# x loaded behind the first quarter of wq, and the last rows of wo in smaller pieces, in a DMA-bound attention kernel

## The chip, the cores and the metric

The kernel runs on one core of one Trainium2 chip. The metric is device microseconds of one execution. Runs of this kernel scatter by a few tenths of a microsecond (363.38 to 363.65 in the first three), so every experiment was run in five rounds beside runs of the kernel before, on the same chip. All runs told of here are fast, with a granted TensorE clock of 1.00 (0.995 at least). A ratio is the mean time of one kernel's fast runs over that of the kernel before in the same rounds, so it is not quite the ratio of the medians that are quoted. In the profiles PE is TensorE (PEld its weight loads), DVE VectorE, ACT ScalarE, POOL GpSimd, and SP the engine that issues the loads; a load is said to have landed when the last step of its semaphore stands in the trace (the kernel before starts on row 28 of wo at 356.86 us, 0.05 us after its landing at 356.81).

## The reference

Grouped-query attention over a cache, with its projections:

```python
# x (32, 4, 1024), k_cache and v_cache (32, 4, 2048, 128), wq (1024, 4096), wo (4096, 1024), all bf16
q = (x @ wq).reshape(B, Sq, Hq, Dh).transpose(0, 2, 1, 3)      # Hq = 32, Dh = 128
k = jnp.repeat(k_cache, 8, axis=1); v = jnp.repeat(v_cache, 8, axis=1)
p = softmax(einsum("bhqd,bhkd->bhqk", q, k) * Dh ** -0.5)
o = einsum("bhqk,bhkd->bhqd", p, v)
return o.transpose(0, 2, 1, 3).reshape(B, Sq, Hq * Dh) @ wo
```

About 151 MB have to be read (64 loads of 2 MB for k and v, 8 MB each for wq and wo), and 128 tokens are all that they are used for.

## The kernel before

All loads are issued from one queue (SP), in program order. First x and the four quarters of wq; x is transposed on TensorE, and the q projection takes one quarter of wq after another:

```python
p.dma("sp", lambda e: e.dma_start(x_sb, x_flat[:, :]), [], "x", "s_x")
wq_v = wq.rearrange("(p a) n -> p a n", p=128)
for c in range(4):
    p.dma("sp", lambda e, c=c: e.dma_start(w_sb[:, 2 * c:2 * c + 2, :], wq_v[:, 2 * c:2 * c + 2, :]),
          [], ("wq", c), f"s_w{c}")
# ... then the loads of k and v, each when its buffer is free
```

x is 256 KB, 2 KB a partition; a quarter of wq is 2 MB, 16 KB a partition. The v buffers lie where wq lies, so the first v load waits for the q projection.

At the end come 32 "rows" of wo (a row is 256 KB, the 128x1024 block of wo for one head), in pieces of up to four rows, into buffers that k and v leave. `WO` counts the rows of a piece; the last row, number 31, comes in two halves of its columns:

```python
WO = (4, 4, 4, 4, 4, 4, 2, 2, 2, 1)
pieces = [(sum(WO[:c]), m, 0, D) for c, m in enumerate(WO)] + [(Hq - 1, 1, 0, NA), (Hq - 1, 1, NA, D)]
# ...
def oproj(u):                        # for u in range(32): two matmuls a row, 512 columns each
    for j, (at, n0, n1) in enumerate(COLS):
        # ... matmul ps_s[:, at:...] += oT(u).T @ wo_row(u)[:, n0:n1]
        piece = next(c for c, (v, m, a, z) in enumerate(pieces) if v <= u < v + m and a <= n0 and n1 <= z)
        p.op("pe", mm, [("wo", piece), ("ot", B - 1)], ("op", j) if u == Hq - 1 else None)
```

A matmul may start when its whole piece has landed. Then ACT and DVE copy a half of the result each, and two DMAs store them.

## Time and profile before

Median 363.38 us. The page's rows of 40 slices: the DMA row is the mean busy share of the 16 DMA engines in tenths, the other what they moved.

```profile
DMA  8999999999999999999999999999999999999995
GB/s 328 429 431 433 429 428 420 431 428 428 425 422 435 426 429 424 432 428 431 426 424 435 425 431 424 429 431 429 429 424 431 429 429 424 428 433 428 412 414 197
```

The engines are busy, 9 tenths or more, from the second slice to the last but one. So the time is the start of the stream, plus the bytes at about 427 GB/s, plus what comes after the last bytes. Loads are issued long before they land, as the table of DMA issues shows (size, then microseconds from issue to landing):

```profile
big<-in_wo_dram SPq DMA_DIRECT2D x6, 1024.0 KB, 22.8
big<-in_wo_dram SPq DMA_DIRECT2D x3, 512.0 KB, 24.5
P_sb<-in_x_dram SPq DMA_DIRECT2D x1, 256.0 KB, 2.7
big<-in_wo_dram SPq DMA_DIRECT2D x1, 256.0 KB, 21.8
big<-in_wo_dram SPq DMA_DIRECT2D x2, 128.0 KB, 19.1
```

Two stretches of the timeline matter. Its columns are start, duration, engine, line, operation and tiles, count, and in brackets the idle time before it and what ended that. First the start:

```profile
0.74 0.38 SPq L186 DMA_DIRECT2D P_sb<-in_x_dram  x1
1.17 1.86 SPq L189 DMA_DIRECT2D big<-in_wq_dram  x4
3.47 1.07 PE L243 MATMUL ps_r<-ident,P_sb 128*128 128x128 bf16 x8 [3.47 <-DMA P_sb<-in_x_dram]
...
8.67 0.59 PE L262 MATMUL ps_r<-big,P_sb 128*128 128x512 bf16 x1 [4.12 <-DMA big<-in_wq_dram]
...
23.26 0.39 PE L262 MATMUL ps_r<-big,P_sb 128*128 128x512 bf16 x1 [1.26 <-DMA big<-in_wq_dram]
...
26.92 0.33 SPq L210 DMA_DIRECT2D big<-in_v_cache_dram  x1
```

PE can start on x at 3.47 us and on the first quarter of wq at 8.67, once each has landed (at 3.43 and 8.53); it waits for the last quarter, too. Then the end. L418 is the matmul of a row's first 512 columns, L16 (a helper) that of the second 512; row 28 starts at 356.86:

```profile
356.06 0.38 PE L418 MATMUL ps_s<-big,KT_sb 128*128 128x512 bf16 x1
356.27 0.38 PE L16 MATMUL ps_s<-big,KT_sb 128*128 128x512 bf16 x1
356.85 0.33 PEld L418 LDWEIGHTS ps_s<-big,KT_sb 128*128 128x128 bf16 x2 [0.91 <-DMA big<-in_wo_dram]
356.86 0.39 PE L418 MATMUL ps_s<-big,KT_sb 128*128 128x512 bf16 x1 [0.21 <-DMA big<-in_wo_dram]
...
357.73 0.38 PE L418 MATMUL ps_s<-big,KT_sb 128*128 128x512 bf16 x1
...
358.38 0.38 PE L16 MATMUL ps_s<-big,KT_sb 128*128 128x512 bf16 x1
358.58 0.60 ACT L427 ACTIVATE P_sb<-ps_s 128x512 bf16<-128x512 f32 x1 [16.24 <-PE ps_s L418]
358.80 0.69 DVE L428 CAST P_sb<-ps_s 128x512 bf16<-128x512 f32 x1 [16.12 <-PE ps_s L16]
```

Matmuls overlap: they start every 0.215 us, though each is shown as 0.38. Row 27 could have been followed at 356.49 (356.27 + 0.215), and row 28 starts 0.37 us after that, when its piece has landed. From there eight matmuls run without a further wait.

### The profile page before, as it was taken

The numbers are of one execution on the slowest core, as the hardware profiler recorded it, in microseconds if no ns is written. First come the engines' busy times: TensorE is split into PE (matmuls) and PEld (weight loads), VectorE is DVE, ScalarE is ACT, GpSimd is POOL, SyncE is SP. The second block draws the span as 40 slices with busy tenths as digits, with TensorE's granted clock in tenths as the row PEclk, the third lists the DMA queues.
The fourth block names the chain that finished last, engine by engine and source line by source line (L and its number), as shares of the span: only waits on it lengthen the run. The fifth ranks groups of instructions, "written<-read, shape, count | busy, mean of one in ns | idle before, by whom it ended". The sixth has DMA issues, their size and how long they took to land. (4 is left out here: it accounts for less than half of the span.)

```text
span 361.8 us, 6210 instructions
## 1 busy us (share of the span) xinstructions
PE 307.2 (85%) x2998; PEld 146.8 (41%) x2338; DVE 269.1 (74%) x170; ACT 102.7 (28%) x110; POOL 165.3 (46%) x262
## 2 busy tenths in 40 slices
PE   1988788999989999988999888888888889889896
PEld 1002000454445544444445444444333344449711
DVE  0018799999899898879998888888888888856500
ACT  1014222333333333333333333333322223333000
POOL 8002055355555555554455444445555554444000
PEclk9999999999999999999999999999999999999999
DMA  8999999999999999999999999999999999999995
GB/s 328 429 431 433 429 428 420 431 428 428 425 422 435 426 429 424 432 428 431 426 424 435 425 431 424 429 431 429 429 424 431 429 429 424 428 433 428 412 414 197
DMA packets 11963, 151.66 MB, mean 419 GB/s; under 512 B 1328, under 2 KB 1840, under 8 KB 2480
## 3 DMA queue, kind: packets, MB, share of 16 engines
q1 hardware_dynamic: 11808, 151.39, 98.7%
q8 instruction: 6, 0.10, 0.1%
q10 hardware_dynamic: 144, 0.13, 0.1%
q14 instruction: 5, 0.04, 0.0%
HBM read 151.26 MB, written 0.26 MB: 419 GB/s over the span
## 5 line engine op out<-in xcount | busy, mean ns | idle before, releaser
L327 DVE STREAM_TRANSPOSE KT_sb<-big 128x2048 f32<-128x2048 f32 x64 | 146.6, 2293 | 16.8 <-DMA big<-in_k_cache_dram 16.8
L353 ACT ACTIVATE P_sb<-ps_s,negmx 128x2048 bf16<-128x2048 f32 x32 | 82.0, 2564 | 185.0 <-DVE negmx L349 185.0
L16 PE MATMUL ps_s<-KT_sb,QD_sb 128*128 128x512 bf16 x384 | 103.7, 377 | 0.0
L384 POOL COPY PD_sb<-PT_sb 32x1024 f32<-32x1024 f32 x62 | 64.1, 1034 | 63.4 <-PE ps_r L393 60.6
L384 POOL COPY big<-PT_sb 32x1024 f32<-32x1024 f32 x61 | 63.0, 1034 | 59.1 <-PE ps_r L393 56.3
L349 DVE TENSOR_REDUCE negmx<-ps_s 128x1 f32<-128x2048 f32 x32 | 73.2, 2286 | 12.4 <-PE ps_s L16 10.9
L393 PE MATMUL ps_r<-big 128*128 128x128 bf16 x1024 | 59.8, 219 | 11.3 <-PEq L85 11.3
L393 PE MATMUL ps_r<-big,PD_sb 128*128 128x128 bf16 x1024 | 59.8, 219 | 9.9 <-PEq L85 9.9
L393 PEld LDWEIGHTS ps_r<-big 128*128 128x128 bf16 x1024 | 57.9, 98 | 22.1 <-issue 21.6
L393 PEld LDWEIGHTS ps_r<-big,PD_sb 128*128 128x128 bf16 x1024 | 58.0, 98 | 21.2 <-issue 20.7
L340 PE MATMUL ps_s<-KT_sb,QD_sb 128*128 128x512 bf16 x128 | 48.3, 377 | 18.3 <-PEq L85 18.3
L340 PEld LDWEIGHTS ps_s<-KT_sb,QD_sb 128*128 128x128 bf16 x128 | 12.3, 96 | 103.1 <-issue 103.1
L362 DVE STREAM_TRANSPOSE PT_sb<-P_sb 128x1024 f32<-128x1024 f32 x32 | 39.8, 1245 | 15.8 <-ACT P_sb L353 15.8
L317 POOL COPY QD_sb<-QT_sb 32x64 f32<-32x64 f32 x128 | 29.4, 229 | 46.1 <-DVE QT_sb L296 20.4
L16 PE MATMUL ps_r<-ident 128*128 128x384 bf16 x173 | 33.3, 325 | 0.0
L365 PEld LDWEIGHTS ps_r<-ssum,permf 128*128 128x128 f32 x64 | 11.9, 187 | 24.8 <-issue 23.1
L402 ACT ACTIVATE QT_sb<-ps_r,rinv 128x128 bf16<-128x128 f32 x32 | 11.7, 367 | 29.5 <-PE ps_r L393 27.3
L278 DVE TENSOR_SCALAR KT_sb<-ps_r 128x512 bf16<-128x512 f32 x2 | 1.3, 686 | 20.1 <-PE ps_r L262 20.1
L16 PE MATMUL ps_s<-big,KT_sb 128*128 128x512 bf16 x32 | 12.1, 379 | 1.2 <-DVE KT_sb L409 1.1
L428 DVE CAST P_sb<-ps_s 128x512 bf16<-128x512 f32 x1 | 0.7, 691 | 16.1 <-PE ps_s L16 16.1
L418 PE MATMUL ps_s<-big,KT_sb 128*128 128x512 bf16 x30 | 11.4, 381 | 1.4 <-DMA big<-in_wo_dram 1.4
L251 PE MATMUL ps_r<-ident 128*128 128x384 bf16 x32 | 10.3, 322 | 0.0
(41 smaller groups left out, 85.3 us busy)
## 6 DMA issues: line engine op xcount, KB each, us to landing
big<-in_k_cache_dram SPq DMA_DIRECT2D x32, 2048.0 KB, 18.6
big<-in_v_cache_dram SPq DMA_DIRECT2D x32, 2048.0 KB, 22.1
big<-in_wq_dram SPq DMA_DIRECT2D x4, 2048.0 KB, 14.0
big<-in_wo_dram SPq DMA_DIRECT2D x6, 1024.0 KB, 22.8
big<-in_wo_dram SPq DMA_DIRECT2D x3, 512.0 KB, 24.5
P_sb<-in_x_dram SPq DMA_DIRECT2D x1, 256.0 KB, 2.7
big<-in_wo_dram SPq DMA_DIRECT2D x1, 256.0 KB, 21.8
big<-in_wo_dram SPq DMA_DIRECT2D x2, 128.0 KB, 19.1
```

Source lines behind the costliest of these rows:

```text
L16: return eng.add_instruction(mybir.InstMatmult(name=nc.get_next_instruction_name(), engine=eng.engine, start_tensor_calc=start, stop_tenso ...
L317: p.op("pool", lambda e, s=src, d=dst: e.tensor_copy(d, s), waits if g == 0 else [("pt", i - 2)] * (g == 1 and i > 1), ("qd", i) if g == G ...
L327: p.op("dve", lambda e, s=src, d=dst: e.transpose(d, s), waits, ("kt", i, c), gives="t_kt" if c else None)
L340: mm = lambda e, a_=(out_, lhsT, rhs), f=first, l=last: e.matmul(a_[0], lhsT=a_[1], rhs=a_[2], start=f, stop=l, skip_group_check=True)
L349: p.op("dve", lambda e: e.tensor_reduce(negmx[:, i % 4:i % 4 + 1], ps_s[:, :], AX.X, ALU.max, negate=True), [("qk", i)], ("negmx", i))
L353: p.op("act", lambda e: e.activation(P_sb[:, :, :, :].rearrange("p t r w -> p t w r"), ps_s[:, :].rearrange("p (t w r) -> p t w r", w=2, r=R),
L362: p.op("dve", lambda e: e.transpose(dst, src), [("exp", i)], ("pt", i))
L365: p.op("pe", lambda e: e.matmul(ring[(i if i == L else i // 2 * 2) % 4][:, 510 + i % 2:511 + i % 2], lhsT=permf[:, :], rhs=ssum[:, i % 4:i ...
L384: p.op("dve" if i >= B - 2 and g < i - B + 4 else "pool", lambda e, s=src, d=dst: e.tensor_copy(d, s), [free] * (g == 0 or i >= B - 2) + [ ...
L393: p.op("pe", lambda e: e.matmul(buf[:, 0:Dh], lhsT=pd_of(i)[:, t // 2, :, :, :, t % 2].rearrange("p x g q -> p (x g q)"), rhs=big[:, slot_ ...
L402: p.op("act", lambda e: e.activation(dst, src, ACT.Copy, scale=rinv[:, i % 4:i % 4 + 1]), [("pv", i), ("rinv", i)], ("o", i))
L418: mm = lambda e, a=(out_, lhsT, rhs): e.matmul(a[0], lhsT=a[1], rhs=a[2], start=(u == 0), stop=(u == Hq - 1), skip_group_check=True)
```

## The change

The intent: start the stream with the large load that the q projection needs first, and let row 28 start when its own 256 KB are there instead of those of row 29 as well.

```diff
-    WO = (4, 4, 4, 4, 4, 4, 2, 2, 2, 1)
+    WO = (4, 4, 4, 4, 4, 4, 2, 2, 1, 1, 1)
 ...
-        p.dma("sp", lambda e: e.dma_start(x_sb, x_flat[:, :]), [], "x", "s_x")
         wq_v = wq.rearrange("(p a) n -> p a n", p=128)
         for c in range(4):
             p.dma("sp", lambda e, c=c: e.dma_start(w_sb[:, 2 * c:2 * c + 2, :], wq_v[:, 2 * c:2 * c + 2, :]),
                   [], ("wq", c), f"s_w{c}")
+            if c == 0:
+                p.dma("sp", lambda e: e.dma_start(x_sb, x_flat[:, :]), [], "x", "s_x")
```

Nothing else moves: on every other engine the instructions and their order are the same, and SP issues one DMA more.

## The prediction

> **What bounds the kernel now.** The DMA engines. The page's row of slices shows the mean DMA share at 9 tenths or more from the second slice to the second last, at 412 to 435 GB/s; PE is busy 85%, DVE 74%. The queue never runs dry: wo pieces land 19 to 24 us after issue (table of DMA issues). So the time is: start of the stream + bytes at about 427 GB/s + what follows the last bytes. Fine windows put the first large completions at 2.3 us and the last bytes at 357.6 us of a 361.8 us span. The chain that ended last agrees: a wo DMA until 356.81, then 1.7 us of matmuls, the copy, the store.
>
> **The end.** The timeline shows the output projection waiting for pieces of wo: row 27 ends its issue near 356.49 (0.215 us a matmul, two a row), row 28 begins at 356.86, when the 512 KB piece of rows 28 and 29 has landed. From there eight matmuls run at their own pace: no further wait. The change splits that piece into two of 256 KB. [...] The previous 512 KB piece landed 1.28 us before this one, so half of it is an estimated 0.6 us: row 28 lands near 356.25, before PE wants it (356.49). Row 29 lands near 356.85 to 356.95, PE wants it at 356.92. Bytes stop at 357.6, so the last halves are there for 357.8 and 358.0. Gain: 0.3 to 0.37 us, all on the chain. Cost: one more issue (about 0.4 us on SP, 17 us ahead of need, free) and 2 KB instead of 4 KB runs for 512 KB, under 0.1 us.
>
> **The start.** x (256 KB) is issued at 0.74 us, wq at 1.17 us; both at full rate: x's bytes and the first wave of wq's 16 KB packets complete back to back (473 KB between 2.3 and 3.1 us), so x in front leaves no visible hole. Moving it behind the first wq load moves the same bytes; I give it 0 us, within 0.3 either way (better start with large packets, or x no longer hidden in the start-up).
>
> On the compute side it costs: x now lands near 8.7 us instead of 3.45. Transposes (1.07 us) and the copy (0.69 us) follow, so the q projection starts near 10.6 instead of 8.67. PE then catches up: it used to idle 1.26 us before the last wq load (23.26 us). The first 16 matmuls run at about 0.42 us each, then 0.215 [...]. The projection ends an estimated 0.4 us later (26.7 to 27.1), v0 is issued at 27.3 instead of 26.92, k3 near 37.3. Bytes issued before k3 last until about 42 us, so 4 us of slack absorb this.
>
> **Sum.** 363.38 - 0.35 (end) + 0.0 (start) = 363.0 us, 8 in 10 within 362.4 to 363.6. Faster by over 2%: 0.005; within 2%: 0.99; slower by over 2%: 0.005.
>
> **What would show it.** Right: no PE wait, or under 0.15 us, before row 28; last bytes to the end of the copies shorter by about 0.3 us; DMA busy throughout; v0 issued later, mean GB/s unchanged. Wrong: a slice near 37 to 45 us with low GB/s (the late q projection starved the queue); row 28 still waiting past 356.8 relative to the stream's end (the small pieces land together, the slowest engine deciding); a start of the stream earlier or later by over 0.3 us[...].

The trace of the kernel before does show the last five pieces of wo landing in the order of their issue, on its timeline at 355.52, 356.81, 357.43, 357.78 and 358.10 us. The cost of the smaller runs can be estimated from the same trace: there a packet of wo of 2 KB took 84 ns and one of 4 KB 162 (medians), so 512 KB in 2 KB packets, eight times two for one on each of 16 engines, take an estimated 0.05 us longer.

## The result, and the profile after

Median 363.35 us (363.28 to 363.52, 6 runs) against 363.48 us (363.38 to 363.65, 6 runs) before: ratio 0.9997, 95% interval 0.9984 to 1.001. The means differ by 0.11 us. The DMA row and its GB/s:

```profile
DMA  8999999999999999999999999999999999999995
GB/s 319 433 435 419 428 433 431 431 412 428 430 428 424 428 429 433 430 419 431 429 431 429 419 431 433 429 422 428 433 429 431 419 431 433 429 429 420 417 415 211
```

Busy throughout, as before; no slice near 40 us is low. The start:

```profile
0.74 0.38 SPq L188 DMA_DIRECT2D big<-in_wq_dram  x1
1.17 0.43 SPq L191 DMA_DIRECT2D P_sb<-in_x_dram  x1
...
8.78 1.07 PE L244 MATMUL ps_r<-ident,P_sb 128*128 128x128 bf16 x8 [8.78 <-DMA P_sb<-in_x_dram]
...
10.63 0.61 PE L263 MATMUL ps_r<-big,P_sb 128*128 128x512 bf16 x1 [0.78 <-DVE P_sb L248]
...
27.12 0.33 SPq L211 DMA_DIRECT2D big<-in_v_cache_dram  x1
```

x lands 5.3 us later, the projection starts 2.0 us later and has caught up to 0.20 us by its end: the first v load is issued at 27.12 for 26.92. And the end (row 28 is the L419 at 356.57):

```profile
356.57 0.38 PE L419 MATMUL ps_s<-big,KT_sb 128*128 128x512 bf16 x1
356.79 0.38 PE L16 MATMUL ps_s<-big,KT_sb 128*128 128x512 bf16 x1
357.01 0.10 PEld L419 LDWEIGHTS ps_s<-big,KT_sb 128*128 128x128 bf16 x1 [0.55 <-DMA big<-in_wo_dram]
...
357.24 0.38 PE L16 MATMUL ps_s<-big,KT_sb 128*128 128x512 bf16 x1
357.65 0.10 PEld L419 LDWEIGHTS ps_s<-big,KT_sb 128*128 128x128 bf16 x1 [0.55 <-DMA big<-in_wo_dram]
357.66 0.39 PE L419 MATMUL ps_s<-big,KT_sb 128*128 128x512 bf16 x1
...
358.00 0.10 PEld L419 LDWEIGHTS ps_s<-big,KT_sb 128*128 128x128 bf16 x1 [0.24 <-DMA big<-in_wo_dram]
358.10 0.38 PE L419 MATMUL ps_s<-big,KT_sb 128*128 128x512 bf16 x1
358.32 0.38 PE L16 MATMUL ps_s<-big,KT_sb 128*128 128x512 bf16 x1
```

Row 28 starts 0.29 us earlier, at PE's own pace. But row 30 (357.66) now starts 0.2 us later than PE's pace after row 29 (357.24 + 0.215) allows: its weights wait for its landing. The weights of row 31 wait for their landing too, but its matmul at 358.10 is again at PE's pace. The last matmul starts at 358.32 for 358.38: of 0.29 us gained at row 28, 0.06 are left.

The trace also records each load's landing: its semaphore counts 16 steps, read here as one from each of the 16 DMA engines (the records do not name the engine). Read out of those records, with all landings counted from the first data packet, which is put at 1.80 us in every run, for this and the later runs:

```
                 third k load      rows 26,27   last half row   start of      from rows 26,27
                 mean of   last    all landed   all landed      last matmul   to last matmul
                 16 eng.   engine
before           37.68     37.95   355.57       358.14          358.38        2.81
x_only           37.89     38.07   355.57       358.13          358.36        2.79
wo_only          37.72     37.93   355.54       358.08          358.14        2.59
wo_only_again    37.78     38.48   355.77       358.39          358.39        2.63
wo_only_third    37.82     38.49   356.04       358.60          358.61        2.57
after            37.91     38.14   355.68       358.32          358.32        2.65
after_again      37.82     38.07   355.47       358.11          358.11        2.65
after_third      37.97     38.24   355.57       358.21          358.21        2.65
wo_coarse        37.73     37.88   355.29       357.82          358.70        3.40
pool_extra       37.86     39.55   356.82       359.40          359.39        2.57
```

(Matmul starts are from the timelines, on which the first data packet stands at 1.75 to 1.77 us. So a landing is 0.03 to 0.05 us earlier on the timeline than in the table, and the last column some 0.04 us too short, in all runs alike.) In the kernel before, the last half had landed 0.28 us before its matmul, both on the timeline; after the change it is 0.04. Row 30 is what PE waits for: in all seven profiles with the new pieces of this table its first matmul starts within 0.05 us of its landing, and the last matmul follows 0.65 to 0.67 us later, three steps at PE's pace. The last half lands 0.04 to 0.10 us before that last matmul, so it leaves hardly any room beyond.

### The profile page after: what moved, and what is told of

Read it like the earlier page. It is cut to its first block, busy times and chain, and to the rows that moved or that the text cites. A ratio compares the mean times of both kernels' runs of the same rounds, so it can differ in the third digit from the quotient of the medians.

```text
span 361.7 us, 6211 instructions
## 1 busy us (share of the span) xinstructions
PE 306.7 (85%) x2998; PEld 146.8 (41%) x2338; DVE 269.1 (74%) x170; ACT 102.8 (28%) x110; POOL 165.5 (46%) x262
## 5 line engine op out<-in xcount | busy, mean ns | idle before, releaser
L419 PE MATMUL ps_s<-big,KT_sb 128*128 128x512 bf16 x30 | 11.4, 381 | 1.2 <-DMA big<-in_wo_dram 1.2
```

What stands on the lines that cost most here:

```text
L419: mm = lambda e, a=(out_, lhsT, rhs): e.matmul(a[0], lhsT=a[1], rhs=a[2], start=(u == 0), stop=(u == Hq - 1), skip_group_check=True)
```

## The experiments

Theory A, formed on this trace: the change has two small effects of opposite sign. The split gains, but only until the landings of row 30 and of the last half take over; and x behind wq delays the stream. Rival B: the start is neutral, and the split eats its gain itself, since smaller pieces land later.

### One half at a time

`x_only` keeps the old pieces:

```diff
-    WO = (4, 4, 4, 4, 4, 4, 2, 2, 1, 1, 1)     # from the changed kernel
+    WO = (4, 4, 4, 4, 4, 4, 2, 2, 2, 1)
```

> Only x behind the first wq load; wo as before. Theory A (two opposite effects): the first wave of 16 KB packets takes about 1.3 us where x's small packets took 1.06 us, and x later costs its own time again, so the third k load lands about 0.2 us later and the run is 0.1 to 0.25 us longer than before. Rival B (the start is neutral, the split eats its own gain): within 0.05 us of before.

`wo_only` is the kernel before with the new `WO` alone:

```diff
-    WO = (4, 4, 4, 4, 4, 4, 2, 2, 2, 1)        # from the kernel before
+    WO = (4, 4, 4, 4, 4, 4, 2, 2, 1, 1, 1)
```

> Only the split of the piece of rows 28 and 29; x first as before. Theory A: row 28 starts without a wait, the start costs nothing, and what is left is bounded by the landing of row 30 and the last halves: 0.1 to 0.25 us shorter than before. Rival B: the smaller runs make the last landings late, so 0 to 0.1 us shorter, as in the whole change.

Measured in the same rounds: `x_only` 363.59 us against 363.56 (means 0.03 us apart, standard error 0.05), `wo_only` 363.34 us (0.20 us shorter, standard error 0.06). So the split gains, against B, and moving x costs the time nothing that can be seen, against A, which expected 0.1 to 0.25 us. The landings speak against B as well: in `wo_only` the smaller pieces are not late, as row 29 lands at 356.85, row 30 at 357.48 and the last half at 358.08, for 356.85, 357.47 and 358.14 before. But A's cause at the start is there in the records: the third k load lands on average over the engines at 37.89 us for 37.68. The one-microsecond windows at the start show where from (columns: window, its length, busy time of PE, PEld, DVE, ACT and POOL, granted clock, DMA share, GB/s; the view counts a packet in the window in which it starts). Before:

```profile
1.00:2.00 1.00, 0.00 (x0) 0.00 (x0) 0.00 (x0) 1.00 (x1) 0.70 (x3) 1.00 0.37 35
2.00:3.00 1.00, 0.00 (x0) 0.00 (x0) 0.00 (x0) 0.01 (x1) 0.88 (x3) 1.00 1.29 440
3.00:4.00 1.00, 0.53 (x5) 0.53 (x6) 0.00 (x0) 0.00 (x0) 1.00 (x1) 1.00 0.76 311
4.00:5.00 1.00, 0.55 (x6) 0.29 (x3) 0.42 (x1) 0.00 (x0) 1.00 (x1) 1.00 1.13 475
```

After:

```profile
1.00:2.00 1.00, 0.00 (x0) 0.00 (x0) 0.00 (x0) 1.00 (x1) 0.70 (x3) 1.00 0.83 180
2.00:3.00 1.00, 0.00 (x0) 0.00 (x0) 0.00 (x0) 0.01 (x1) 0.88 (x3) 1.00 0.50 147
3.00:4.00 1.00, 0.00 (x0) 0.00 (x0) 0.00 (x0) 0.00 (x0) 1.00 (x1) 1.00 1.10 459
4.00:5.00 1.00, 0.00 (x0) 0.00 (x0) 0.00 (x0) 0.00 (x0) 1.00 (x1) 1.00 0.79 328
```

With wq first, only nine packets of 16 KB start in the second of these windows (147 GB/s), because those of the first are still under way. (The prediction read these views as completions; "complete back to back" is "start back to back".) The packet records say why: 11 of the first 16 packets of 16 KB took 1.1 to 1.5 us each, later ones 0.61. That first wave, 16 packets, is 256 KB, as much as x, and was through 1.52 us after the stream's first packet; with x first, all of x was through after 1.30 us (the first packet of wq started after 1.04, about the 1.06 us of the expectation). x's first packets were slow too, 0.17 to 0.60 us each for 0.08 later. To compare at equal bytes: the 16 packets that follow the first 512 KB started on average 1.86 to 1.93 us after the first packet in seven profiles with x first, and 1.95 to 2.06 in the four with x behind one load. So a slow first wave was paid either way here, it was about 0.1 us cheaper with small packets, and this is most of what the order costs the stream.

### x one place further back: is there slack?

```diff
-            if c == 0:                          # from the changed kernel
+            if c == 1:
                 p.dma("sp", lambda e: e.dma_start(x_sb, x_flat[:, :]), [], "x", "s_x")
```

(`WO` is the changed kernel's here; the expectation says "wo as before", which was a slip and is worth 0.1 to 0.2 us.)

> x behind the second wq load, wo as before: x lands some 5 us later again, near 13.7 us. The q projection then ends near 32 us and k3 is issued near 42 us, which is when the bytes issued before it run out (about 4 to 5 us of slack). If the slack is as I read it, a hole of 0.5 to 2 us in the DMA row near 42 to 44 us, and the run 0.5 to 2 us longer. If the slack is larger than read, within 0.3 us of the kernel with x behind one load.

364.65 us median (364.25 to 365.36), against 363.56: 1.27 us longer in the mean. The first v load is issued at 32.08 us and the fourth k load at 42.06 us, and the queue runs dry, as these windows of this run show:

```profile
40.00:42.00 2.00, 1.86 (x9) 0.29 (x3) 2.00 (x1) 0.00 (x0) 0.00 (x0) 1.00 0.94 401
42.00:44.00 2.00, 2.00 (x12) 0.19 (x2) 0.23 (x2) 0.00 (x0) 0.17 (x1) 1.00 0.74 139
44.00:46.00 2.00, 2.00 (x14) 0.00 (x0) 2.00 (x1) 0.00 (x0) 0.06 (x1) 1.00 0.83 336
```

(139 + 336) GB/s over 2 us each is 0.95 MB where 430 GB/s would have moved 1.72 MB: 1.8 us of stream lost (this profiled run, 365.20 us, was 1.65 us above the mean of before). About half of it is an empty queue: the last 16 packets before the pause ended at 42.28 us on average, the first 16 after it began at 43.19. The rest is a slow restart, as these took 0.9 to 1.7 us each for 0.61 later; so here the slow first wave came after the pause as well. The slack that the prediction read, about 4 us, is real, and the change (0.20 us late) is well inside it.

### The pieces taken the other way

```diff
-    WO = (4, 4, 4, 4, 4, 4, 2, 2, 2, 1)
+    WO = (4, 4, 4, 4, 4, 4, 2, 2, 3)
```

> x first; rows 28, 29 and 30 land as one piece of 768 KB, so the split is taken the other way. If the chain of the end is landing of the piece, then PE at its own pace, row 28 waits until row 30 used to land, 0.62 us later than before, and the run is 0.5 to 0.65 us longer. If something else (the last half's landing, the copies) sets the end, under 0.2 us longer.

364.01 us, 0.43 us longer in the mean, just under the 0.5 to 0.65 expected. Row 28 waits for all of rows 28 to 30:

```profile
356.00 0.38 PE L16 MATMUL ps_s<-big,KT_sb 128*128 128x512 bf16 x1
357.18 0.39 PE L418 MATMUL ps_s<-big,KT_sb 128*128 128x512 bf16 x1 [0.80 <-DMA big<-in_wo_dram]
```

and the last matmul starts at 358.70, seven steps of 0.215 us later, though the last half had landed at 357.82. From rows 26 and 27 it is 3.40 us, 0.59 more than before (in this run rows 26 and 27 landed 0.28 us early). In this direction the chain is what the prediction said: the landing of row 28's piece, then PE's pace.

### The whole change against the split, again, and two attempts to do better

`after_again` and `wo_only_again` are the two kernels unchanged.

> The whole change again, in the same rounds as the split alone. If x behind the first wq load costs something under the finer tail (the tail can no longer hide it), 0.05 to 0.15 us longer than the split alone; if x's place costs nothing, equal to it within 0.05 us. Against before: 0.1 to 0.2 us shorter.

> The split alone again, for the comparison in the same rounds: 0.15 to 0.3 us shorter than before, as in its first run (0.22).

`x_act` is the split with x issued from ACT's queue, so that neither waits for the other's issue (x at 0.73 us and the first wq load at 0.74, where SP alone issued them at 0.74 and 1.17):

```diff
-        p.dma("sp", lambda e: e.dma_start(x_sb, x_flat[:, :]), [], "x", "s_x")
+        p.dma("act", lambda e: e.dma_start(x_sb, x_flat[:, :]), [], "x", "s_x")
```

> The split, with x issued from the ACT queue and the four wq loads from SP at the same moment. The bytes are the same and the stream's first packets come at 1.8 us as before, so the time equals the split alone within 0.1 us. If what counts is how early wq's descriptors stand in the queue, the third k load lands 0.2 us or more earlier and the run is as much shorter.

`fine` is the split with the last row in three pieces and the last half copied out in two parts (the third part is written to columns of ps_s of its own, from 1024 on; the form with both parts in the same 512 columns was not run):

```diff
-    COLS = ((0, 0, NA), (NA, NA, D))
+    NB = 768
+    COLS = ((0, 0, NA), (NA, NA, NB), (2 * NA, NB, D))
...
-            p.op("dve", lambda e: e.tensor_copy(y_sb[:, NA:D], ps_s[:, NA:D]), [("op", 1)], ("oe", 1))
+            p.op("dve", lambda e: e.tensor_copy(y_sb[:, NA:NB], ps_s[:, NA:NB]), [("op", 1)])
+            p.op("dve", lambda e: e.tensor_copy(y_sb[:, NB:D], ps_s[:, 2 * NA:2 * NA + D - NB]), [("op", 2)], ("oe", 1))
```

> The split, and the last row of wo in pieces of 512, 256 and 256 columns, with the last 512 columns copied out in two parts. The last landing is the same, but only a 256-column matmul (about 0.11 us) and a 256-column copy (about 0.4 us for 0.69) follow it: 0.1 to 0.4 us shorter than the split alone if the chain of the end is last landing, matmul, copy; if row 30's landing and PE's pace bind instead, 0 to 0.15 us shorter.

Against 363.43 us before (mean 363.47): `after_again` 363.37 (0.06 us shorter in the mean), `wo_only_again` 363.35 (0.09 shorter), `x_act` 363.44 (0.02 shorter), `fine` 363.44 (0.11 shorter), each with a standard error of 0.05 to 0.08. None can be told from another. `after_again` and `wo_only_again` fell short of what was expected against before (0.1 to 0.2 and 0.15 to 0.3 us). `fine` is 0.02 us shorter than the split alone, so it is the second branch of its expectation that fits (0 to 0.15). The 256-column steps were as short as expected: the next matmul starts 0.11 us later (354.81 to 354.92), and the two copies take 0.42 and 0.41 us for 0.69. `x_act` met its expectation in the time, 0.07 us from the split alone, but x did not come early: PE could start on it at 8.92 us, as late as behind a quarter of wq. The packet records show x's 128 packets of 2 KB taking turns about one for one with 16 KB packets of wq (127 of them start in the same time), from 2.6 to 8.3 us.

What stands out in the table is another thing: `wo_only_again` is the same kernel as `wo_only`, and its last half landed 0.31 us later, though the third k load's mean over the engines was only 0.06 us later. What had moved was the slowest engine.

### Does one late DMA engine set the end?

The page of the kernel before lists its DMA queues (packets, MB, share of 16 engines' span), two of them of kind "instruction":

```profile
q1 hardware_dynamic: 11808, 151.39, 98.7%
q8 instruction: 6, 0.10, 0.1%
...
q14 instruction: 5, 0.04, 0.0%
```

q8 has six packets of 16 KB; those of q14 are of 8 KB. In the kernel before, the engines of a load finish within 0.48 us of each other until the first of those of 16 KB. After it (56.6 us) the last engine is 1.51 us behind the middle one, for 0.27 at the load before, after the second (71.6 us) two are, and at the last loads the last engine comes in 1.9 us after the first. The packet itself took 1.02 us, and the lag grew by 1.24. Theory: these packets run on the same DMA engines as the loads, and the engine that was held up most decides when a load has landed. To test it, POOL got 400 instructions for nothing, in time in which it idles (that more instructions bring more such packets was the guess):

```diff
         p.op("pool", lambda e: e.memset(words(PF_sb.rearrange("p t x g q w -> p (t x g q w)")), 0.0), [], "pf0")
+        pad = sbuf("pad", [128, 400], F32)
+        for c in range(400):
+            p.op("pool", lambda e, c=c: e.memset(pad[:, c:c + 1], 0.0), [], None, chain=False)
```

> The split alone, with 400 one-column memsets on POOL in its idle time near 10 to 28 us, which nothing waits for. Theory: the instruction packets of 16 KB (6 of them in every trace) each delay one DMA engine, and the engine that was delayed most decides the last landing. Then one or two more such packets appear, one engine falls behind by 0.6 to 1.3 us more, and the run is 0.3 to 1.2 us longer than the split alone. Rival: the delay is shared by all engines (16 KB over 16 engines is under 0.05 us); then the time is within 0.1 us of the split alone.

365.00 us (364.93 to 365.06), 1.45 us longer than before and 1.56 us longer than the split alone in the same rounds: more than expected. The packets were not the ones expected either: the 16 KB ones stayed six, and three of 8 KB came on the other instruction queue, at 14.6, 19.4 and 24.4 us, as this run's page counts:

```profile
q8 instruction: 6, 0.10, 0.1%
...
q14 instruction: 8, 0.07, 0.0%
```

The last engine of a load is 0.27 us behind the middle one before the first of them, and 0.47, 1.13 and 1.79 after the first, second and third. The third k load's mean over the engines is 37.86 us, hardly changed, and its last engine 39.55. And at the end the windows of this run show the last engine alone:

```profile
357.00:357.50 0.50, 0.50 (x4) 0.10 (x1) 0.00 (x0) 0.00 (x0) 0.00 (x0) 1.00 0.43 152
357.50:358.00 0.50, 0.50 (x4) 0.10 (x1) 0.00 (x0) 0.00 (x0) 0.00 (x0) 1.00 0.07 25
358.00:358.50 0.50, 0.50 (x4) 0.10 (x1) 0.00 (x0) 0.00 (x0) 0.00 (x0) 1.00 0.06 23
358.50:359.00 0.50, 0.50 (x4) 0.10 (x1) 0.00 (x0) 0.00 (x0) 0.00 (x0) 1.00 0.05 18
```

A DMA share of 0.06 is one engine of sixteen. For a microsecond and a half, 15 of them have nothing left to do, and the kernel waits. POOL's own work held nobody up: its memsets were over at 24.2 us, and its next work waited for DVE until 31.27. That the memsets disturbed the loads in some other way than by these packets is not excluded by a run of its own, but the delay came in steps at the three packets and on the last engine, not on the mean. Not all of the 1.56 us is this delay: the last matmul starts 0.8 to 1.25 us later than in the three profiles of the split alone, and at the very end POOL takes 0.37 us for 0.08 between its last two semaphore instructions, 0.29 us that the late engine does not explain.

### The two once more

> The whole change a third time, in the same rounds as the split alone: the mean of the 16 engines' landings of the third k load about 0.13 us later than with x first (37.87 for 37.74 us from the stream's first packet at 1.80), and the time 0 to 0.1 us longer than the split alone.

> The split alone a third time: 0.1 to 0.2 us shorter than before; from the landing of rows 26 and 27 to the start of the last matmul about 2.6 us, where before has 2.8.

Against 363.46 us before (mean 363.55): `after_third` 363.40 (0.16 us shorter in the mean), `wo_only_third` 363.41 (0.11 shorter, with one run at 363.80, which is the profiled one). Three comparisons each now: the whole change is 0.11, 0.06 and 0.16 us shorter than before, the split alone 0.20, 0.09 and 0.11. Every one of them points the same way; alone, only the first one of the split is well clear of its standard error (0.20 for 0.06). Pooled with weights by their standard errors, the whole change is 0.10 us shorter (standard error 0.04) and the split alone 0.15 (0.04). So a small gain is real, and between the two there is no difference to be seen. `after_third` had its third k load at 37.97 in the mean for the 37.87 expected, and was 0.05 us shorter than the split alone where 0 to 0.1 longer was expected, which is within the noise.

## Why the prediction was right or wrong

The time, 363.35 us, is in the range (362.4 to 363.6), and "within 2%" was right. But the kernel before, at 363.48 us, lies in that range too, so this alone says little; of the 0.35 us forecast, 0.11 came. Point by point:

- **DMA bounds the kernel, and the queue stays full.** Right: the DMA row, and `x_third`, which emptied the queue by 5 us more delay and lost 1.27 us.
- **The compute side of moving x.** Right: PE could start on x at 8.78 us (said: 8.7), the projection started at 10.63 (10.6), the first v load was issued at 27.12 (27.3), the fourth k load at 37.09 (37.3). The projection ended 0.20 us later, not 0.4. The prediction's two paces of the matmuls, 0.42 us and then 0.215, are in the traces: 0.43 us from one 512-column matmul of the projection to the next at first, then 0.215. The slow pace lasted for 14 matmuls before and 12 after the change; over all profiles it was 8 to 14, so x's place does not decide it.
- **The start of the stream, "0 us, within 0.3 either way".** Right in the time (0.03 us, standard error 0.05), but not because nothing happened. With x second, the mean over the engines of the third k load's landing is 37.82 to 37.97 us in four profiles, with x first 37.68 to 37.82 in six (those of the table without `pool_extra`, and `fine` with 37.77): about 0.15 us later. The landing of a load's last engine does not show it, as that engine's own delay scatters by more.
- **Row 28 starts without a wait.** Right, at 356.57, right behind row 27, and 0.29 us earlier than before.
- **"Gain: 0.3 to 0.37 us, all on the chain".** This is the term that was mis-sized. Measured against the landing of rows 26 and 27, the last matmul came 2.81 us later before and 2.57 to 2.65 us in the seven profiles with the new pieces: about 0.19 us gained. In the device time it was 0.06 to 0.20 us. The step that failed is what comes after row 28: the prediction let PE run on at its own pace to the end ("Bytes stop at 357.6, so the last halves are there for 357.8 and 358.0") and did not ask when row 30 lands. All on the timeline of the kernel before: row 30 landed at 357.43, for a PE that would have wanted it at 357.35 (356.49 and four steps of 0.215). PE started 0.05 us after the landing it waited for (row 28 here, 356.81 and 356.86; row 30 after the change, 357.61 and 357.66), so 357.48 for row 30 and 358.13 for the last matmul, which was at 358.38: with these landings 0.25 us was the most to be had, and the old trace said so. The last half allowed no more: the last data packet ended at 357.62, but the load had landed only at 358.10, 0.5 us after the last bytes. So the wait moved from row 28 to row 30, with the last half right behind it.
- **"The small pieces land together, the slowest engine deciding"** stood among the things that would make the prediction wrong. It holds in part: the pieces landed one after another (after the change rows 28 to 30 at 356.35, 357.01 and 357.66 us, as in the table), but each only with its last engine, 1.7 to 1.8 us after its first. In `pool_extra` this engine came to be 1.79 us behind the middle one, and the last matmul started 0.8 to 1.25 us later.

What stays open: why the slowest engine's delay differs from run to run of one kernel (its share of the third k load landed at 37.93 or 38.49 us), and so whether x's place is worth 0.05 us one way or the other. The landings do show when it arises. In `wo_only_again` and `wo_only_third` the last engine is already 0.76 and 0.72 us behind the middle one when the first wq load lands (0.14 to 0.40 in all other profiles) and stays so until 53 us; after the first 16 KB packet the lag is 1.46 us in the one and 2.26 in the other. That the packet hit the engine which was late already, in the one with the larger number, is a guess: as the records name no engine, it is not shown. No version found beats both kernels clearly; the split alone is the smaller change and does as well as the whole.

## What to carry to other kernels

Splitting the last load gained here only until the next landing took over (0.29 us at row 28, 0.06 of it left at the last matmul): read when each of the last pieces has landed, not when bytes stop, and put those times beside PE's own pace. Here a load was there only with its slowest DMA engine (the last half row of the kernel before 1.9 us after the first engine had its share), so look at the spread over the engines; 400 instructions that nothing waits for lengthened this DMA-bound kernel by 1.56 us, with three more instruction packets. Putting a large load in front of a small one did not start the stream faster here: the first packets were slow in both orders (up to 0.60 us for 0.08 with 2 KB, up to 1.5 for 0.61 with 16 KB).
